# Linear attention on one core: GpSimd's two helper operations tied to VectorE's reciprocal and product of three heads back, with new instruction orders

## The chip, the cores and the metric

The kernel runs on one core of one Trainium2 chip. The metric is the device time of one execution in microseconds. The core has five engines with queues of their own: TensorE (PE, with its weight loads as PEld), VectorE (DVE), ScalarE (ACT), GpSimd (POOL) and SyncE (SP), which here only issues transfers. The profile reports a span from the first to the last instruction, which is not the time.

## The reference, cut to what matters

Inputs q, k, v are bf16 of shape 1 x 32 x 2048 x 128: 32 heads, 2048 rows, 128 columns.

```python
phi_q = where(q > 0, q + 1, exp(q)) + 1e-6
phi_k = where(k > 0, k + 1, exp(k)) + 1e-6
kv  = einsum("bhsd,bhse->bhde", phi_k, v)
z   = einsum("bhsd->bhd", phi_k)
num = einsum("bhqd,bhde->bhqe", phi_q, kv)
den = einsum("bhqd,bhd->bhq", phi_q, z)[..., None] + 1e-6
out = num / den
```

The kernel uses phi(x) = relu(x) + (min(exp(x), 1) + 1e-6) and feeds the two terms to TensorE as two accumulated products.

## The kernel before

A head is 16 tiles of 128 rows. Each engine executes a fixed list of named operations, and a semaphore wait is put before an operation for each dependency in another list. The names, with head `h` (and part) as a suffix:

- ScalarE: `ek` exp(k), `eq` exp(q), `rqa` relu of 8 q tiles, `kvs` copies the kv sums out of PSUM.
- VectorE: `em` and `emq` are min(., 1) + 1e-6 on exp(k) and exp(q); `rkd` is relu of 8 k tiles. All three read and write SBUF. `rqb` is relu of 8 q tiles, `r` the reciprocal of the denominators, `f` the product numerator times reciprocal; these three read PSUM. `r{h}.0` and `f{h}.0` cover 12 tiles, `r{h}.1` and `f{h}.1` four.
- GpSimd: `rkp` is relu of the other 8 k tiles, `v1` copies v beside a column of ones.
- TensorE: `T` transposes q, `kv` is the product of phi(k) and v (below: the v-product), `n` the product of phi(q) and kv.
- SyncE: `ldq`, `ldk`, `ldv` load, `st` stores.

```python
def gate(name, h):          # extra dependencies of v1 and rkp
    return []

ORDER = {
    "DVE": """
        # ... cut ...
        emq8.0 f7.0 rkd10.0 em10.0 r7.1 rqb9 f7.1 r8.0 emq9.0 f8.0 rkd11.0 em11.0 r8.1 rqb10 f8.1 r9.0 rkd12.0 f9.0
        emq10.0 em12.0 r9.1 rqb11 f9.1 r10.0 f10.0 emq11.0 em13.0 rkd13.0 r10.1 rqb12 f10.1 rkd14.0 r11.0 emq12.0
        # ... cut ...
    """,
    "POOL": """
        ident0 ident rkp0.0 rkp1.0 v10.1 v10.0 v11.0 v12.0 rkp2.0 rkp3.0 v13.0 v14.0 rkp5.0 rkp4.0 v15.0 rkp6.0
        # ... cut ...
    """,   # "PE", "ACT" and "SP" likewise
}
# ... cut: inside head(h) ...
add("DVE", f"em{h}.{i}", lambda e, a=a, b=b: e.tensor_scalar(
    em_sb[:, h % NE, a:b], em_sb[:, h % NE, a:b], 1.0, EPS, op0=ALU.min, op1=ALU.add), [f"ek{h}.{i}"])
add("POOL", f"rkp{h}.{i}", lambda e, a=a, b=b: e.tensor_scalar(
    rk_sb[:, h % NR, a:b], k_sb[:, h % NI, a:b], BIG, 0.0, op0=ALU.min, op1=ALU.max),
    over("ldk", h, k_parts, a, b) + freed(NR, h, ("kv", kv_parts)) + gate("rkp", h))
add("POOL", f"v1{h}.{i}", lambda e, a=a, b=b: e.tensor_copy(
    v1_sb[:, h % NV, a:b, 0:D].bitcast(i32), v_sb[:, h % NI, a:b].bitcast(i32)),
    [f"ldv{h}.{i}"] + freed(NV, h, ("kv", kv_parts)) + gate("v1", h))
# ... cut ...
```

Without a gate, `v1` and `rkp` of head h can start when their loads have landed and the v-product of head h - 2 has freed their buffers.

Of the kernel before, what the change touches and what calls it, by code (L numbers as in the profile page):

```python
# [12 lines left out]
HALVES = ((0, 8), (8, 16))  # L13
WHOLE = ((0, 16),)
# [7 lines left out]


def kv_parts(h):
    return WHOLE


RKP = (8, 8, 8, 8, 8, 8, 8, 8, 8, 8, 8, 8, 8, 8, 8, 8, 8, 8, 8, 8, 8, 8, 8, 8, 8, 8, 8, 8, 8, 8, 8, 8)
# [23 lines left out]


def gate(name, h):
    return []


ORDER = {
    "PE": """
        T0.0 T0.1 w1 w0 T1.0 kv0.0 kv1.0 n0.0 n0.1 T2.0 kv2.0 n1.0 T3.0 n1.1 kv3.0 n2.0 T4.0 n2.1 kv4.0 n3.0 T5.0  # L60
        n3.1 kv5.0 n4.0 T6.0 n4.1 kv6.0 n5.0 n5.1 T7.0 kv7.0 n6.0 T8.0 n6.1 kv8.0 n7.0 T9.0 n7.1 kv9.0 n8.0 T10.0
        n8.1 kv10.0 n9.0 T11.0 n9.1 kv11.0 n10.0 T12.0 n10.1 kv12.0 n11.0 T13.0 n11.1 kv13.0 n12.0 T14.0 n12.1
        kv14.0 n13.0 T15.0 n13.1 kv15.0 n14.0 T16.0 n14.1 kv16.0 n15.0 T17.0 n15.1 kv17.0 n16.0 n16.1 T18.0 kv18.0
        n17.0 T19.0 n17.1 kv19.0 n18.0 T20.0 n18.1 kv20.0 n19.0 T21.0 n19.1 kv21.0 n20.0 T22.0 n20.1 kv22.0 n21.0
        T23.0 n21.1 kv23.0 n22.0 T24.0 n22.1 kv24.0 n23.0 n23.1 T25.0 kv25.0 n24.0 T26.0 n24.1 kv26.0 n25.0 T27.0
        n25.1 kv27.0 n26.0 T28.0 n26.1 kv28.0 n27.0 T29.0 n27.1 kv29.0 n28.0 T30.0 n28.1 kv30.0 n29.0 T31.0 n29.1
        kv31.0 n30.0 n30.1 n31.1 n31.0 n31.2
    """,
    "DVE": """
        v1ones0 rkd0.0 em0.1 rkd1.0 rqb0 em0.0 eps0 em1.0 emq0.1 emq0.0 rqb1 v1ones1 eps1 rkd2.0 eps2 ones emq1.0  # L70
        rkd3.0 em2.0 r0.0 f0.0 em3.0 rqb2 r0.1 rkd4.0 f0.1 r1.0 emq2.0 f1.0 em4.0 rkd5.0 r1.1 rqb3 f1.1 r2.0 f2.0
        emq3.0 em5.0 rkd6.0 rqb4 r2.1 f2.1 r3.0 emq4.0 f3.0 em6.0 r3.1 rqb5 rkd7.0 f3.1 r4.0 emq5.0 f4.0 em7.0 r4.1
        f4.1 rqb6 r5.0 f5.0 emq6.0 rkd8.0 em8.0 r5.1 rqb7 f5.1 r6.0 emq7.0 f6.0 rkd9.0 em9.0 r6.1 rqb8 f6.1 r7.0
        emq8.0 f7.0 rkd10.0 em10.0 r7.1 rqb9 f7.1 r8.0 emq9.0 f8.0 rkd11.0 em11.0 r8.1 rqb10 f8.1 r9.0 rkd12.0 f9.0
        emq10.0 em12.0 r9.1 rqb11 f9.1 r10.0 f10.0 emq11.0 em13.0 rkd13.0 r10.1 rqb12 f10.1 rkd14.0 r11.0 emq12.0
# [137 lines left out]
def bass_standalone__linear_attn_elu__prompt_kernel(nc: bass.Bass, q: bass.AP, k: bass.AP, v: bass.AP, out: bass.AP):  # L213
# [11 lines left out]
    with ExitStack() as es:  # L225
# [73 lines left out]
        def head(h):  # L299
# [21 lines left out]
            for i, (a, b) in enumerate(v_parts(h)):  # L321
# [131 lines left out]
```

## Time and profile before

| | before |
|---|---|
| time, runs known at the prediction | 176.82 us median (176.76 to 179.11) |
| the profiled run | 179.61 us, span 177.8, granted clock 0.989 |
| first steady v-product (head 2) to the last (head 31) | 20.99 to 163.97 us, 29 periods |
| steady period where nothing is late | 4.73 us |

"Steady" below means from 21 us on.

The page of the kernel before: busy time of each engine with its share of the span and number of instructions, the rate of the transfers in 40 equal slices, and the chain of work that ended last.

```profile
span 177.8 us, 6416 instructions
...
PE 161.9 (91%) x2842; PEld 158.1 (89%) x2842; DVE 158.4 (89%) x266; ACT 154.4 (87%) x131; POOL 71.5 (40%) x71
...
GB/s 171 323 407 416 411 404 406 412 404 410 408 406 409 406 417 411 407 411 417 412 417 414 420 414 416 416 414 417 412 405 418 414 196 183 285 417 412 418 313 120
...
PE 43%; DVE 20%; DMA 18%; issue 5%; SPq 4%; ACT 4%; POOL 3%; DVEq 0%; POOLq 0%
```

Three engines are within a few per cent of each other, and the chain runs through TensorE more than through any other (43%). The rate falls to 196, 183 and 285 GB/s in three slices near 142 to 156 us. The next view is busy time in one stretch, 130 us of the steady part (columns: stretch, length, then busy us of each engine with its count of instructions, the granted TensorE clock, the share of the transfer engines, GB/s).

```profile
core 0: us, PE busy (x) PEld busy (x) DVE busy (x) ACT busy (x) POOL busy (x), PEclk, DMA share, GB/s
21.00:151.00 130.00, 126.36 (x2272) 124.51 (x2273) 127.74 (x210) 125.56 (x105) 58.45 (x53) 1.00 0.99 397
```

VectorE is the busiest, although it does no more work than 4.6 us per head (its eight operations from start to start). The reason shows in the timeline of the kernel before (start, duration, engine, line, operation, operands; in brackets the idle time before and what ended it). In this kernel L311 is `em`, L314 `rkd`, L318 `rkp`, L352 `rqb`.

```profile
140.29 0.68 DVE L311 TENSOR_SCALAR la<-la 128x2048 bf16<-128x2048 bf16 x1
140.58 1.29 POOL L318 TENSOR_SCALAR la<-la 128x1024 bf16<-128x1024 bf16 x1 [2.42 <-PE la L329]
140.89 1.25 DVE L314 TENSOR_SCALAR la<-la 128x1024 bf16<-128x1024 bf16 x1
...
142.16 0.65 DVE L352 TENSOR_SCALAR la<-la 128x1024 bf16<-128x1024 bf16 x1
```

GpSimd's relu was ready in the middle of `em`. It waited for the rest of it (its record is 1.29 us instead of 1.04), and the following `rkd` took 1.25 us instead of its usual 0.42. `rqb` at 142.16 overlaps the next GpSimd copy and keeps its usual 0.65. Counting every `em`, `emq` and `rkd` that is more than 0.15 us above its usual duration (0.68, 0.68, 0.42), the steady part has 8 of them, together 5.0 us. These are called stretched operations below.

### The profile page before, as it was taken

How to read it: one execution, taken by the hardware profiler on the slowest of the kernel's cores; microseconds unless marked ns; L12 is line 12 of the kernel's file. 1: busy time of each engine (PE TensorE's matmuls, PEld its weight loads, DVE VectorE, ACT ScalarE, POOL GpSimd, SP SyncE). 2: the span in 40 equal slices, each digit the busy share in tenths (PEclk: the TensorE clock that was granted, in tenths of full speed). 3: DMA queues.
4: the chain of work that ended last, by engine and by line, in shares of the span. 5: the costliest groups of instructions: out<-in, count | busy, mean ns of one | idle time of the engine just before them, and what ended most of it. 6: DMA issues, size and time to landing. Idle time of an engine off the chain costs nothing.

```text
span 177.8 us, 6416 instructions
## 1 busy us (share of the span) xinstructions
PE 161.9 (91%) x2842; PEld 158.1 (89%) x2842; DVE 158.4 (89%) x266; ACT 154.4 (87%) x131; POOL 71.5 (40%) x71
## 2 busy tenths in 40 slices
PE   2986999999999999999889999988999989999870
PEld 1976999999999999999789999978999889989770
DVE  0156899999999999998999999999999999989973
ACT  2599799999999999999898999978999979994600
POOL 1253818417454246262723626264256424360000
PEclk9999999999999999999999999999999999999968
DMA  5999999999999999999999999999999945999973
GB/s 171 323 407 416 411 404 406 412 404 410 408 406 409 406 417 411 407 411 417 412 417 414 420 414 416 416 414 417 412 405 418 414 196 183 285 417 412 418 313 120
DMA packets 19179, 67.52 MB, mean 380 GB/s; under 512 B 2128, under 2 KB 2512, under 8 KB 19152
## 3 DMA queue, kind: packets, MB, share of 16 engines
q1 hardware_dynamic: 19152, 67.12, 95.1%
q8 instruction: 22, 0.36, 0.8%
q14 instruction: 5, 0.04, 0.1%
HBM read 50.33 MB, written 16.78 MB: 377 GB/s over the span
## 4 chain that ended last, share of the span: by engine, by line
PE 43%; DVE 20%; DMA 18%; issue 5%; SPq 4%; ACT 4%; POOL 3%; DVEq 0%; POOLq 0%
PE la L329 17%; DMA la<-in_k_dram 11%; PE la L364 9%; PE la L366 8%; PE la L340 8%; DVE la L380 8%; DMA out_dram<-la 7%; SPq L296 4%; DVE la L314 4%; DVE la L311 3%; DVE la L352 2%; ACT la L343 2%; DVE la L345 2%; POOL la L318 2%; POOL la L322 2%
## 5 line engine op out<-in xcount | busy, mean ns | idle before, releaser
L380 DVE TENSOR_TENSOR la<-la 128x1536 bf16<-128x1536 f32 (+2 forms) x65 | 77.7, 1199 | 2.0 <-DMA out_dram<-la 1.4
L366 PE MATMUL la<-la 128*128 128x129 bf16 x512 | 69.2, 222 | 0.0
L364 PE MATMUL la<-la 128*128 128x129 bf16 x512 | 69.1, 221 | 0.0
L329 PE MATMUL la<-la 128*128 128x129 bf16 x1024 | 64.0, 219 | 2.0 <-ACT la L349 1.4
L343 ACT ACTIVATE la<-la 128x2048 bf16<-128x2048 bf16 (+1 forms) x33 | 60.1, 1825 | 6.5 <-PE la L366 6.0
L308 ACT ACTIVATE la<-la 128x2048 bf16<-128x2048 bf16 (+1 forms) x33 | 61.3, 1860 | 2.1 <-DMA la<-in_k_dram 1.9
L329 PEld LDWEIGHTS la<-la 128*128 128x128 bf16 x1024 | 59.9, 97 | 2.7 <-DVE la L278 1.5
L318 POOL TENSOR_SCALAR la<-la 128x1024 bf16<-128x1024 bf16 x32 | 36.1, 1137 | 44.1 <-PE la L329 33.5
L322 POOL COPY la<-la 128x1024 int32<-128x1024 int32 (+1 forms) x33 | 35.3, 1076 | 44.0 <-PE la L329 22.4
L366 PEld LDWEIGHTS la<-la 128*128 128x128 bf16 x512 | 50.0, 98 | 0.0
L364 PEld LDWEIGHTS la<-la 128*128 128x128 bf16 x512 | 47.8, 98 | 0.0
L340 PE MATMUL la<-la 128*128 128x128 bf16 x512 | 34.8, 222 | 7.0 <-DMA la<-in_q_dram 3.6
L340 PEld LDWEIGHTS la<-la 128*128 128x128 bf16 x512 | 29.6, 99 | 9.0 <-issue 4.0
L359 PE MATMUL la<-la 128*128 128x3 bf16 (+1 forms) x192 | 32.6, 170 | 2.5 <-DVE la L380 2.5
L349 ACT ACTIVATE la<-la 128x1024 bf16<-128x1024 bf16 x32 | 32.6, 1019 | 2.5 <-PE la L340 2.5
L311 DVE TENSOR_SCALAR la<-la 128x2048 bf16<-128x2048 bf16 (+1 forms) x33 | 23.3, 706 | 3.1 <-ACT la L308 3.1
L314 DVE TENSOR_SCALAR la<-la 128x1024 bf16<-128x1024 bf16 x32 | 18.0, 566 | 7.4 <-DMA la<-in_k_dram 7.3
L345 DVE TENSOR_SCALAR la<-la 128x2048 bf16<-128x2048 bf16 (+1 forms) x33 | 22.3, 677 | 0.4 <-ACT la L343 0.4
L359 PEld LDWEIGHTS la<-la 128*128 128x128 bf16 x192 | 18.9, 99 | 3.5 <-DVE la L380 3.1
L352 DVE TENSOR_SCALAR la<-la 128x1024 bf16<-128x1024 bf16 x32 | 21.3, 667 | 0.7 <-ACT la L343 0.7
L373 DVE RECIPROCAL la<-la 128x12 f32<-128x12 f32 (+2 forms) x65 | 12.8, 198 | 2.2 <-PE la L366 1.4
L334 ACT ACTIVATE la<-la 128x129 bf16<-128x129 f32 x32 | 9.0, 281 | 1.0 <-PE la L329 1.0
(14 smaller groups left out, 13.5 us busy)
## 6 DMA issues: line engine op xcount, KB each, us to landing
la<-in_k_dram SPq DMA_DIRECT2D x31, 512.0 KB, 13.9
la<-in_q_dram SPq DMA_DIRECT2D x31, 512.0 KB, 13.9
la<-in_v_dram SPq DMA_DIRECT2D x31, 512.0 KB, 13.3
out_dram<-la SPq DMA_DIRECT2D x31, 512.0 KB, 13.2
la<-in_q_dram SPq DMA_DIRECT2D x2, 256.0 KB, 3.0
la<-in_k_dram SPq DMA_DIRECT2D x2, 256.0 KB, 5.2
la<-in_v_dram SPq DMA_DIRECT2D x2, 256.0 KB, 7.6
out_dram<-la SPq DMA_DIRECT2D x2, 192.0 KB, 2.1
```

The lines of the kernel that those rows point to most:

```text
L308: add("ACT", f"ek{h}.{i}", lambda e, a=a, b=b: e.activation(em_sb[:, h % NE, a:b], k_sb[:, h % NI, a:b], ACT.Exp), [f"ldk{h}.{i}"] + freed ...
L311: add("DVE", f"em{h}.{i}", lambda e, a=a, b=b: e.tensor_scalar(em_sb[:, h % NE, a:b], em_sb[:, h % NE, a:b], 1.0, EPS, op0=ALU.min, op1=AL ...
L318: add("POOL", f"rkp{h}.{i}", lambda e, a=a, b=b: e.tensor_scalar(rk_sb[:, h % NR, a:b], k_sb[:, h % NI, a:b], BIG, 0.0, op0=ALU.min, op1=A ...
L322: add("POOL", f"v1{h}.{i}", lambda e, a=a, b=b: e.tensor_copy(v1_sb[:, h % NV, a:b, 0:D].bitcast(i32), v_sb[:, h % NI, a:b].bitcast(i32)), ...
L329: ins = e.matmul(kv_ps, lhsT=src[:, j], rhs=v1_sb[:, h % NV, j, 0:NC], start=(j + part == 0), stop=(j == NT - 1 and part == 1))
L340: ins = e.transpose(xT[:, j], q_sb[:, h % NI, j], ident[:])
L343: add("ACT", f"eq{h}.{i}", lambda e, a=a, b=b: e.activation(emq_sb[:, h % NQ, a:b], xT[:, a:b], ACT.Exp), [f"T{h}.{i}"] + freed(NQ, h, ("n ...
L349: add("ACT", f"rqa{h}", lambda e: e.activation(rq_sb[:, h % NQ, 0:n], xT[:, 0:n], ACT.Relu), over("T", h, q_parts, 0, n) + freed(NQ, h, (" ...
L359: e.matmul(_ap(o_ps[:, :], o + D, [[NC, m]]), lhsT=ones[:], rhs=epsr[:, 0:m], start=True, stop=False, skip_group_check=True)
L364: e.matmul(to, lhsT=emq_sb[:, h % NQ, t], rhs=kvs_sb[:, h % NK], start=False, stop=False, skip_group_check=True)
L366: ins = e.matmul(to, lhsT=rq_sb[:, h % NQ, t], rhs=kvs_sb[:, h % NK], start=False, stop=True, skip_group_check=True)
L380: return e.tensor_tensor(out=_ap(o_sb[:, :, :, :], first(o_sb[:, h % NO, t0, 0:1]) - first(o_sb[:, :, :, :]), [[m * D, nb], [D, m], [1, D] ...
```

## The change

Its apparent intent (the kernel's text does not say): let GpSimd start at a moment when VectorE reads from PSUM, so that the two do not meet. It makes four changes: the gates; the v-product in two halves; GpSimd and the stores in head order; and new orders for all engines.

```diff
 def kv_parts(h):
-    return WHOLE
+    return HALVES
...
 def gate(name, h):
-    return []
+    if h < 3:
+        return []
+    return [f"r{h - 3}.0"] if name == "v1" else [f"f{h - 3}.0"]
...
     "DVE": """
...
-        emq8.0 f7.0 rkd10.0 em10.0 r7.1 rqb9 f7.1 r8.0 emq9.0 f8.0 rkd11.0 em11.0 r8.1 rqb10 f8.1 r9.0 rkd12.0 f9.0
-        emq10.0 em12.0 r9.1 rqb11 f9.1 r10.0 f10.0 emq11.0 em13.0 rkd13.0 r10.1 rqb12 f10.1 rkd14.0 r11.0 emq12.0
+        rkd10.0 emq8.0 f7.0 em10.0 r7.1 rqb9 f7.1 emq9.0 r8.0 rkd11.0 f8.0 em11.0 r8.1 rqb10 f8.1 emq10.0 r9.0
+        rkd12.0 f9.0 em12.0 r9.1 rqb11 f9.1 r10.0 rkd13.0 f10.0 emq11.0 em13.0 r10.1 rqb12 f10.1 r11.0 emq12.0 f11.0
...
     "POOL": """
-        ident0 ident rkp0.0 rkp1.0 v10.1 v10.0 v11.0 v12.0 rkp2.0 rkp3.0 v13.0 v14.0 rkp5.0 rkp4.0 v15.0 rkp6.0
+        ident0 ident v10.0 rkp0.0 v10.1 rkp1.0 v11.0 v12.0 rkp2.0 v13.0 rkp3.0 v14.0 rkp4.0 v15.0 rkp5.0 v16.0
...
     (PE, ACT and SP reordered as well)
```

More of the change, by code (lines that the diff above doesn't have):

```diff
@@ L54, in gate @@
 def gate(name, h):
-    return []
+    if h < 3:
+        return []
+    return [f"r{h - 3}.0"] if name == "v1" else [f"f{h - 3}.0"]
 ORDER = {
     "PE": """
-        T0.0 T0.1 w1 w0 T1.0 kv0.0 kv1.0 n0.0 n0.1 T2.0 kv2.0 n1.0 T3.0 n1.1 kv3.0 n2.0 T4.0 n2.1 kv4.0 n3.0 T5.0
-        n3.1 kv5.0 n4.0 T6.0 n4.1 kv6.0 n5.0 n5.1 T7.0 kv7.0 n6.0 T8.0 n6.1 kv8.0 n7.0 T9.0 n7.1 kv9.0 n8.0 T10.0
-        n8.1 kv10.0 n9.0 T11.0 n9.1 kv11.0 n10.0 T12.0 n10.1 kv12.0 n11.0 T13.0 n11.1 kv13.0 n12.0 T14.0 n12.1
-        kv14.0 n13.0 T15.0 n13.1 kv15.0 n14.0 T16.0 n14.1 kv16.0 n15.0 T17.0 n15.1 kv17.0 n16.0 n16.1 T18.0 kv18.0
-        n17.0 T19.0 n17.1 kv19.0 n18.0 T20.0 n18.1 kv20.0 n19.0 T21.0 n19.1 kv21.0 n20.0 T22.0 n20.1 kv22.0 n21.0
-        T23.0 n21.1 kv23.0 n22.0 T24.0 n22.1 kv24.0 n23.0 n23.1 T25.0 kv25.0 n24.0 T26.0 n24.1 kv26.0 n25.0 T27.0
-        n25.1 kv27.0 n26.0 T28.0 n26.1 kv28.0 n27.0 T29.0 n27.1 kv29.0 n28.0 T30.0 n28.1 kv30.0 n29.0 T31.0 n29.1
-        kv31.0 n30.0 n30.1 n31.1 n31.0 n31.2
+        w1 T0.0 T0.1 w0 kv0.0 T1.0 kv0.1 kv1.0 kv1.1 n0.0 n0.1 T2.0 kv2.0 kv2.1 n1.0 T3.0 n1.1 kv3.0 kv3.1 n2.0 T4.0
+        n2.1 kv4.0 kv4.1 n3.0 T5.0 n3.1 kv5.0 kv5.1 n4.0 T6.0 n4.1 kv6.0 kv6.1 n5.0 n5.1 T7.0 kv7.0 kv7.1 n6.0 T8.0
+        n6.1 kv8.0 kv8.1 n7.0 T9.0 n7.1 kv9.0 kv9.1 n8.0 T10.0 n8.1 kv10.0 kv10.1 n9.0 T11.0 n9.1 kv11.0 kv11.1
+        n10.0 T12.0 n10.1 kv12.0 kv12.1 n11.0 T13.0 n11.1 kv13.0 kv13.1 n12.0 T14.0 n12.1 kv14.0 kv14.1 n13.0 T15.0
+        n13.1 kv15.0 kv15.1 n14.0 T16.0 n14.1 kv16.0 kv16.1 n15.0 T17.0 n15.1 kv17.0 kv17.1 n16.0 T18.0 n16.1 kv18.0
+        kv18.1 n17.0 T19.0 n17.1 kv19.0 kv19.1 n18.0 T20.0 n18.1 kv20.0 kv20.1 n19.0 T21.0 n19.1 kv21.0 kv21.1 n20.0
+        T22.0 n20.1 kv22.0 kv22.1 n21.0 T23.0 n21.1 kv23.0 kv23.1 n22.0 T24.0 n22.1 kv24.0 kv24.1 n23.0 T25.0 n23.1
+        kv25.0 kv25.1 n24.0 T26.0 n24.1 kv26.0 kv26.1 n25.0 n25.1 T27.0 kv27.0 kv27.1 n26.0 T28.0 n26.1 kv28.0
+        kv28.1 n27.0 T29.0 n27.1 kv29.0 kv29.1 n28.0 T30.0 n28.1 kv30.0 kv30.1 n29.0 T31.0 n29.1 kv31.0 kv31.1 n30.0
+        n30.1 n31.0 n31.1 n31.2
@@ L68 @@
     """,
     "DVE": """
-        v1ones0 rkd0.0 em0.1 rkd1.0 rqb0 em0.0 eps0 em1.0 emq0.1 emq0.0 rqb1 v1ones1 eps1 rkd2.0 eps2 ones emq1.0
-        rkd3.0 em2.0 r0.0 f0.0 em3.0 rqb2 r0.1 rkd4.0 f0.1 r1.0 emq2.0 f1.0 em4.0 rkd5.0 r1.1 rqb3 f1.1 r2.0 f2.0
-        emq3.0 em5.0 rkd6.0 rqb4 r2.1 f2.1 r3.0 emq4.0 f3.0 em6.0 r3.1 rqb5 rkd7.0 f3.1 r4.0 emq5.0 f4.0 em7.0 r4.1
-        f4.1 rqb6 r5.0 f5.0 emq6.0 rkd8.0 em8.0 r5.1 rqb7 f5.1 r6.0 emq7.0 f6.0 rkd9.0 em9.0 r6.1 rqb8 f6.1 r7.0
-        emq8.0 f7.0 rkd10.0 em10.0 r7.1 rqb9 f7.1 r8.0 emq9.0 f8.0 rkd11.0 em11.0 r8.1 rqb10 f8.1 r9.0 rkd12.0 f9.0
@@ L75 @@
-        emq10.0 em12.0 r9.1 rqb11 f9.1 r10.0 f10.0 emq11.0 em13.0 rkd13.0 r10.1 rqb12 f10.1 rkd14.0 r11.0 emq12.0
-        f11.0 em14.0 r11.1 rqb13 f11.1 r12.0 f12.0 emq13.0 rkd15.0 em15.0 r12.1 rqb14 f12.1 rkd16.0 r13.0 emq14.0
-        f13.0 em16.0 r13.1 rqb15 f13.1 r14.0 f14.0 emq15.0 em17.0 rkd17.0 r14.1 rqb16 f14.1 r15.0 rkd18.0 f15.0
-        emq16.0 em18.0 r15.1 f15.1 rqb17 r16.0 f16.0 emq17.0 em19.0 rkd19.0 r16.1 rqb18 f16.1 r17.0 emq18.0 f17.0
-        rkd20.0 em20.0 r17.1 rqb19 f17.1 r18.0 f18.0 emq19.0 rkd21.0 em21.0 r18.1 rqb20 f18.1 r19.0 emq20.0 f19.0
@@ L80 @@
-        em22.0 rkd23.0 rkd22.0 rqb21 r19.1 r20.0 f19.1 f20.0 emq21.0 em23.0 rkd24.0 rqb22 r20.1 f20.1 r21.0 emq22.0
-        f21.0 em24.0 rqb23 r21.1 f21.1 r22.0 emq23.0 rkd25.0 f22.0 em25.0 r22.1 f22.1 rqb24 r23.0 f23.0 emq24.0
-        rkd26.0 em26.0 r23.1 rqb25 f23.1 r24.0 emq25.0 f24.0 em27.0 rkd27.0 r24.1 rqb26 f24.1 r25.0 emq26.0 f25.0
-        rkd28.0 em28.0 r25.1 rqb27 f25.1 r26.0 emq27.0 f26.0 rkd29.0 em29.0 r26.1 rqb28 f26.1 r27.0 emq28.0 f27.0
-        rkd30.0 em30.0 r27.1 rqb29 f27.1 r28.0 f28.0 emq29.0 rkd31.0 em31.0 rqb30 r28.1 f28.1 r29.0 emq30.0 f29.0
@@ L85 @@
-        emq31.0 r29.1 rqb31 r30.0 f29.1 f30.0 r30.1 f30.1 r31.1 f31.1 r31.0 r31.2 f31.0 f31.2
+        eps0 ones rkd0.0 v1ones1 v1ones0 rkd1.0 em0.0 emq0.0 eps2 rqb0 eps1 em0.1 em1.0 rqb1 emq0.1 emq1.0 rkd2.0
+        em2.0 rkd3.0 r0.0 f0.0 em3.0 rkd4.0 r0.1 rqb2 f0.1 r1.0 f1.0 emq2.0 em4.0 r1.1 rqb3 f1.1 emq3.0 r2.0 rkd5.0
+        f2.0 em5.0 r2.1 rqb4 f2.1 r3.0 rkd6.0 emq4.0 f3.0 em6.0 r3.1 rqb5 f3.1 r4.0 rkd7.0 f4.0 emq5.0 em7.0 r4.1
+        f4.1 rqb6 emq6.0 r5.0 rkd8.0 f5.0 em8.0 rqb7 r5.1 f5.1 r6.0 emq7.0 rkd9.0 f6.0 em9.0 r6.1 rqb8 f6.1 r7.0
@@ new lines @@
+        rkd10.0 emq8.0 f7.0 em10.0 r7.1 rqb9 f7.1 emq9.0 r8.0 rkd11.0 f8.0 em11.0 r8.1 rqb10 f8.1 emq10.0 r9.0
+        rkd12.0 f9.0 em12.0 r9.1 rqb11 f9.1 r10.0 rkd13.0 f10.0 emq11.0 em13.0 r10.1 rqb12 f10.1 r11.0 emq12.0 f11.0
+        rkd14.0 em14.0 r11.1 rqb13 f11.1 rkd15.0 r12.0 emq13.0 f12.0 em15.0 rqb14 r12.1 f12.1 r13.0 emq14.0 f13.0
+        em16.0 rkd16.0 r13.1 rqb15 f13.1 r14.0 emq15.0 rkd17.0 f14.0 em17.0 r14.1 rqb16 f14.1 r15.0 rkd18.0 emq16.0
+        f15.0 em18.0 r15.1 rqb17 f15.1 r16.0 emq17.0 f16.0 rkd19.0 em19.0 r16.1 rqb18 f16.1 emq18.0 r17.0 rkd20.0
@@ new lines @@
+        f17.0 em20.0 r17.1 rqb19 f17.1 r18.0 rkd21.0 f18.0 emq19.0 em21.0 r18.1 rqb20 f18.1 r19.0 rkd22.0 f19.0
+        emq20.0 em22.0 rqb21 r19.1 f19.1 r20.0 rkd23.0 f20.0 emq21.0 em23.0 rkd24.0 rqb22 r20.1 f20.1 r21.0 f21.0
+        emq22.0 em24.0 r21.1 rqb23 f21.1 r22.0 rkd25.0 f22.0 emq23.0 em25.0 r22.1 rqb24 f22.1 r23.0 emq24.0 f23.0
+        em26.0 rkd26.0 rqb25 r23.1 f23.1 emq25.0 rkd27.0 r24.0 f24.0 em27.0 r24.1 f24.1 rqb26 r25.0 f25.0 emq26.0
+        em28.0 rqb27 r25.1 f25.1 emq27.0 rkd28.0 r26.0 f26.0 em29.0 r26.1 rqb28 f26.1 rkd29.0 r27.0 emq28.0 f27.0
@@ L86 @@
+        em30.0 r27.1 rqb29 f27.1 rkd30.0 r28.0 emq29.0 f28.0 r28.1 rqb30 f28.1 r29.0 emq30.0 em31.0 rkd31.0 f29.0
+        emq31.0 rqb31 r29.1 f29.1 r30.0 f30.0 r30.1 f30.1 r31.0 f31.0 r31.1 f31.1 r31.2 f31.2
     """,
     "ACT": """
-        rqa0 ek0.1 ek0.0 eq0.1 eq0.0 ek1.0 eq1.0 kvs0 rqa1 ek2.0 kvs1 ek3.0 eq2.0 kvs2 rqa2 ek4.0 eq3.0 kvs3 rqa3
+        eq0.0 eq0.1 ek0.0 rqa0 ek1.0 ek0.1 eq1.0 kvs0 ek2.0 kvs1 rqa1 ek3.0 eq2.0 kvs2 rqa2 ek4.0 eq3.0 kvs3 rqa3
         ek5.0 eq4.0 kvs4 rqa4 ek6.0 eq5.0 kvs5 rqa5 ek7.0 eq6.0 kvs6 rqa6 ek8.0 eq7.0 kvs7 rqa7 ek9.0 eq8.0 kvs8
@@ L92 @@
         ek18.0 eq17.0 kvs17 rqa17 ek19.0 eq18.0 kvs18 rqa18 ek20.0 eq19.0 kvs19 rqa19 ek21.0 eq20.0 kvs20 rqa20
-        ek22.0 eq21.0 rqa21 kvs21 ek23.0 eq22.0 kvs22 rqa22 ek24.0 eq23.0 kvs23 rqa23 ek25.0 eq24.0 kvs24 rqa24
+        ek22.0 eq21.0 kvs21 rqa21 ek23.0 eq22.0 rqa22 kvs22 ek24.0 eq23.0 kvs23 rqa23 ek25.0 eq24.0 kvs24 rqa24
         ek26.0 eq25.0 kvs25 rqa25 ek27.0 eq26.0 kvs26 rqa26 ek28.0 eq27.0 kvs27 rqa27 ek29.0 eq28.0 kvs28 rqa28
@@ L97 @@
     "POOL": """
-        ident0 ident rkp0.0 rkp1.0 v10.1 v10.0 v11.0 v12.0 rkp2.0 rkp3.0 v13.0 v14.0 rkp5.0 rkp4.0 v15.0 rkp6.0
-        v16.0 v17.0 v18.0 rkp7.0 rkp8.0 rkp9.0 v19.0 rkp10.0 v110.0 rkp11.0 v111.0 v112.0 rkp13.0 rkp12.0 v113.0
-        v114.0 rkp15.0 rkp14.0 v115.0 rkp16.0 v117.0 v116.0 rkp17.0 rkp18.0 v119.0 v118.0 rkp19.0 rkp20.0 v121.0
-        v120.0 rkp21.0 v122.0 rkp23.0 rkp22.0 v123.0 rkp24.0 v124.0 v125.0 v126.0 rkp25.0 rkp26.0 rkp27.0 v127.0
-        rkp28.0 v128.0 rkp29.0 v129.0 rkp30.0 rkp31.0 v130.0 v131.0
+        ident0 ident v10.0 rkp0.0 v10.1 rkp1.0 v11.0 v12.0 rkp2.0 v13.0 rkp3.0 v14.0 rkp4.0 v15.0 rkp5.0 v16.0
@@ L103 @@
+        rkp6.0 v17.0 rkp7.0 v18.0 rkp8.0 v19.0 rkp9.0 v110.0 rkp10.0 v111.0 rkp11.0 v112.0 rkp12.0 v113.0 rkp13.0
+        v114.0 rkp14.0 v115.0 rkp15.0 v116.0 rkp16.0 v117.0 rkp17.0 v118.0 rkp18.0 v119.0 rkp19.0 v120.0 rkp20.0
+        v121.0 rkp21.0 v122.0 rkp22.0 v123.0 rkp23.0 v124.0 rkp24.0 v125.0 rkp25.0 v126.0 rkp26.0 rkp27.0 v127.0
+        v128.0 rkp28.0 v129.0 rkp29.0 v130.0 rkp30.0 v131.0 rkp31.0
     """,
     "SP": """
-        ldq0.0 ldq0.1 ldk0.0 ldk0.1 ldk1.0 ldq1.0 ldv0.1 ldv0.0 ldv1.0 ldk2.0 ldv2.0 ldk3.0 ldq2.0 ldv3.0 ldq3.0
@@ L106 @@
-        ldk4.0 ldq8.0 ldv4.0 ldk5.0 ldq4.0 ldv5.0 ldk6.0 ldk7.0 ldq5.0 ldv6.0 ldq6.0 ldv8.0 ldk8.0 ldv7.0 ldq7.0
-        ldk9.0 ldq9.0 ldk11.0 ldq12.0 ldq11.0 ldv9.0 ldk10.0 ldq10.0 ldk14.0 ldv10.0 ldq13.0 ldk15.0 ldk12.0 ldv11.0
-        ldk13.0 ldv13.0 ldv12.0 ldv15.0 ldv14.0 st0.0 ldq14.0 ldq17.0 ldq16.0 ldv16.0 ldq15.0 ldq18.0 ldk16.0
-        ldq19.0 ldv20.0 ldv17.0 ldk18.0 st1.0 st2.0 ldk17.0 st4.0 ldk19.0 ldv19.0 ldv18.0 st3.0 ldv21.0 ldv22.0
-        st5.0 st6.0 st10.0 ldk20.0 ldk22.0 ldv23.0 ldq20.0 ldk21.0 ldq21.0 st9.0 ldk23.0 st7.0 ldq22.0 st8.0 ldq23.0
@@ L111 @@
-        ldk24.0 ldv25.0 ldq26.0 ldq27.0 ldk25.0 ldv24.0 ldk26.0 ldq24.0 st11.0 ldk27.0 ldv26.0 ldq28.0 ldq25.0
-        st14.0 ldq30.0 st12.0 ldv27.0 ldk28.0 st13.0 ldk29.0 ldv28.0 st15.0 ldk30.0 st17.0 ldv29.0 ldq29.0 st18.0
-        st25.0 ldv30.0 ldk31.0 st16.0 ldv31.0 st21.0 ldq31.0 st23.0 st20.0 st24.0 st27.0 st26.0 st28.0 st19.0 st22.0
-        st29.0 st30.0 st31.1 st31.0 st31.2
+        ldq0.0 ldq0.1 ldk0.0 ldv0.0 ldk0.1 ldk1.0 ldv0.1 ldq1.0 ldv1.0 ldk2.0 ldv2.0 ldk3.0 ldq2.0 ldk4.0 ldq3.0
@@ new lines @@
+        ldv3.0 ldv4.0 ldk5.0 ldq4.0 ldv5.0 ldk6.0 ldv6.0 ldq5.0 ldk7.0 ldq6.0 ldk8.0 ldv7.0 ldq7.0 ldq8.0 ldk9.0
+        ldv8.0 ldv9.0 ldk10.0 ldq9.0 ldv10.0 ldq10.0 ldk11.0 ldk12.0 ldv11.0 ldv12.0 ldq11.0 ldv13.0 ldq12.0 st0.0
+        ldv14.0 ldq13.0 ldk13.0 st1.0 ldv15.0 ldk14.0 ldk15.0 ldk16.0 ldq14.0 ldv16.0 ldv17.0 ldk17.0 ldq15.0
+        ldv18.0 st2.0 ldk18.0 ldq16.0 ldq17.0 ldq18.0 st3.0 ldq19.0 st4.0 st5.0 st6.0 ldv19.0 ldq20.0 ldk19.0
+        ldk20.0 ldv20.0 ldk21.0 ldv21.0 ldq21.0 ldv22.0 ldk22.0 st7.0 ldv23.0 ldk23.0 ldq22.0 ldv24.0 ldk24.0 st8.0
@@ L115 @@
+        ldv25.0 st9.0 ldk25.0 ldq23.0 ldq24.0 st10.0 ldk26.0 ldq25.0 st11.0 ldk27.0 ldv26.0 ldq26.0 ldv27.0 st12.0
+        ldk28.0 st13.0 st14.0 ldq27.0 ldv28.0 ldk29.0 st15.0 ldk30.0 ldq28.0 ldv29.0 st16.0 ldq29.0 ldv30.0 ldq30.0
+        st17.0 ldk31.0 ldv31.0 ldq31.0 st18.0 st19.0 st20.0 st21.0 st22.0 st23.0 st24.0 st25.0 st26.0 st27.0 st28.0
+        st29.0 st30.0 st31.0 st31.1 st31.2
     """,
```

## The prediction

> **What bounds the kernel now.** In the steady state a head takes 4.73 us (timeline). TensorE and ScalarE are both 10.0 of 10 us busy between 50 and 80 us (busy time by stretch), so both set this period. VectorE is hardly looser: its eight operations, start to start, add to about 4.6 us. The first steady v-product starts at 20.99 us, after q of head 2 has landed (about 19.8); the last, of head 31, at 164.13. Twenty-nine periods of 4.725 are 137.0, measured 143.1: 6.1 us are lost. The tail from there is 13.7. Where the 6.1 went: VectorE blocked by GpSimd, seen as relu(k) of 1.26 us instead of 0.42 (90.66, 120.88, 140.89) and em or emq of 1.1 instead of 0.68 (85.24, 137.60, 148.04, 159.91), eight in all, about 5 us; products waiting for an output store, 0.86 and 0.53; and the transfer queue, which stood 15.7 us on stores issued too early (the slices at 142 to 156 us move 196, 183 and 285 GB/s instead of 410), so that k of head 31 lands at 156.9 and TensorE and ScalarE lose about 2.
>
> The Trainium skill, "SBUF — State Buffer", section "Who interferes with whom": VectorE and GpSimd share a port pair; who issues first holds it for the whole instruction. The trace agrees: 0.83 us lost per relu(k) against a GpSimd operation of 1.04. It also shows who wins: where GpSimd arrives in the middle of one such VectorE operation and another follows directly (8.75, 115.14, 140.58), GpSimd goes next and the second is blocked.
>
> **What the change does.** No arithmetic is added; kv comes in halves. Stores are issued in head order, after their data are ready: the transfer hole (about 2.4 us) and the store waits (1.4) should go. The start is bound by the same tenth transfer (q of head 2), so it gains little. The gates start the v copy at the end of a 12-tile reciprocal and relu(k) at the end of the 12-tile product. Where one SBUF-to-SBUF operation stands there, followed by work from PSUM, the copy (1.04) hides under the product (1.67) and relu(k) under reciprocal, relu(q), 4-tile product (1.27). But in the new order two such operations stand in a row in 17 places from head 3 on (after r3, r6, r7, r14, r15; after f4, f10, f11, f13, f16, f18 to f23, f25): there the gate puts GpSimd exactly between them, an estimated 0.84 us each, up to 14 us, against VectorE's slack of about 0.13 per head. With none of these collisions the sum is 21 + 137 + 13.7 = 171.7 profiled (170.7 timed); with all of them about 183. A searched order would hardly keep 17 at full price, so I stand between.
>
> **Predicted: 175.5 us, range 170 to 182. Chances: faster by over 2% 0.36, within 2% 0.42, slower by over 2% 0.22.**
>
> **What would show it.** Right: no transfer slice under 390 GB/s between 10 and 150 us; no product waiting for a store; GpSimd waiting for VectorE, not TensorE; the v copies inside the 12-tile products; em, emq or relu(k) stretched by about 0.84 at the 17 places, more VectorE busy time than 158.4. Wrong: VectorE's em, emq, relu(k) all at 0.68, 0.69, 0.42, so GpSimd yields; then the time is near 171.
>
> **What would make it wrong.** GpSimd waking later or yielding (faster); TensorE waiting for a late v1 or relu(k) half (slower); late v loads in the first ten heads.

## The result, and the profile after

The changed kernel takes 184.61 us median (184.51 to 184.76, 4 runs) against 177.13 for the kernel before in the same rounds: a ratio of 1.0399, 95% interval 1.032 to 1.0478, slower. A ratio here is the mean time of one kernel's fast runs over that of the other's fast runs of the same rounds, so it is not quite the ratio of the medians. All runs of the changed kernel were at a granted clock of 0.997 or more.

The page of the changed kernel, the same parts as before:

```profile
span 182.8 us, 6466 instructions
...
PE 163.9 (90%) x2842; PEld 158.3 (87%) x2842; DVE 166.8 (91%) x266; ACT 155.2 (85%) x131; POOL 81.7 (45%) x71
...
GB/s 160 293 414 413 406 408 410 411 405 406 410 405 419 412 411 412 414 410 417 416 415 406 420 412 420 409 417 418 414 419 415 415 420 414 353 177 118 118 185 161
...
DVE 68%; ACT 10%; issue 9%; PE 6%; DMA 4%; SPq 1%; DVEq 0%
DVE la L384 30%; DVE la L349 10%; DVE la L315 9%; DVE la L356 8%; ACT la L347 6%; DVE la L318 6%; DVE la L377 4%; DMA la<-in_k_dram 4%; PE la L344 2%; ACT la L312 2%; ACT la L353 2%; SPq L300 1%; PE la L333 1%; PE la L368 1%; PE la L370 1%
```

The hole in the transfers is gone, and after the first two the slices stay above 400 GB/s until the last load has landed at 152.2 us. But VectorE has 8.4 us more busy time with the same 266 instructions, and the chain of work now runs through VectorE for 68% of the span (20% before). Busy time in the same stretch of 130 us:

```profile
core 0: us, PE busy (x) PEld busy (x) DVE busy (x) ACT busy (x) POOL busy (x), PEclk, DMA share, GB/s
21.00:151.00 130.00, 121.29 (x2150) 117.47 (x2148) 129.32 (x200) 119.86 (x101) 64.67 (x52) 1.00 1.03 413
```

VectorE is busy for 129.3 of 130 us and finishes 200 instructions where it finished 210 before; TensorE has fallen from 126.4 to 121.3 us. The waits of GpSimd in the changed kernel (us in total, times, longest) show that the gates are what it now waits for; L326 is `v1`, L322 `rkp`, L377 the reciprocal, L384 the product:

```profile
POOL la L326 <- DVE la L377: 38.5, 25, 3.1
POOL la L322 <- DVE la L384: 33.1, 27, 4.6
POOL la L326 <- DMA la<-in_v_dram: 12.0, 4, 6.3
POOL la L326 <- PE la L333: 1.6, 1, 1.6
```

The timeline of the changed kernel at `f10.0 emq11.0 em13.0`; L349 is `emq`, L315 `em`, L356 `rqb`:

```profile
69.69 1.74 DVE L384 TENSOR_TENSOR la<-la 128x1536 bf16<-128x1536 f32 x1
71.35 0.68 DVE L349 TENSOR_SCALAR la<-la 128x2048 bf16<-128x2048 bf16 x1
71.52 1.41 POOL L322 TENSOR_SCALAR la<-la 128x1024 bf16<-128x1024 bf16 x1 [0.85 <-DVE la L384]
71.95 1.53 DVE L315 TENSOR_SCALAR la<-la 128x2048 bf16<-128x2048 bf16 x1
73.40 0.17 DVE L377 RECIPROCAL la<-la 128x4 f32<-128x4 f32 x1
73.49 0.65 DVE L356 TENSOR_SCALAR la<-la 128x1024 bf16<-128x1024 bf16 x1
```

The product ends at 71.43 and opens the gate. By then `emq` has started (71.35), so GpSimd waits. When `emq` is done, GpSimd goes next and `em`, the second operation in the row, takes 1.53 us instead of 0.68. Such stretched operations number 18 in the steady part, together 15.1 us; 17 of them stand exactly at the 17 places the prediction lists, at 0.83 to 0.85 us each, and the eighteenth (at 25.97 us) is behind f1.

Put together, the 182.8 us are 19.6 to the v-product of head 2, 150.6 from there to that of head 31 (170.21), and 12.6 after it. Before, the same three were 21.0, 143.0 and 13.8. TensorE's v-product never waits for GpSimd in the changed kernel's list of waits, so the gates do not cost by making TensorE's inputs late.

### The profile page after: what moved, and what is told of

It reads as the page before. It is cut to its first block, busy times and chain, and to the rows that moved or that the text cites. A ratio compares the mean times of both kernels' runs of the same rounds, so it can differ in the third digit from the quotient of the medians.

```text
span 182.8 us, 6466 instructions
## 1 busy us (share of the span) xinstructions
PE 163.9 (90%) x2842; PEld 158.3 (87%) x2842; DVE 166.8 (91%) x266; ACT 155.2 (85%) x131; POOL 81.7 (45%) x71
## 4 chain that ended last, share of the span: by engine, by line
DVE 68%; ACT 10%; issue 9%; PE 6%; DMA 4%; SPq 1%; DVEq 0%
DVE la L384 30%; DVE la L349 10%; DVE la L315 9%; DVE la L356 8%; ACT la L347 6%; DVE la L318 6%; DVE la L377 4%; DMA la<-in_k_dram 4%; PE la L344 2%; ACT la L312 2%; ACT la L353 2%; SPq L300 1%; PE la L333 1%; PE la L368 1%; PE la L370 1%
## 5 line engine op out<-in xcount | busy, mean ns | idle before, releaser
L384 DVE TENSOR_TENSOR la<-la 128x1536 bf16<-128x1536 f32 (+2 forms) x65 | 77.8, 1197 | 0.7
L347 ACT ACTIVATE la<-la 128x2048 bf16<-128x2048 bf16 (+1 forms) x33 | 60.1, 1825 | 16.0 <-PE la L370 11.1
L370 PE MATMUL la<-la 128*128 128x129 bf16 x512 | 68.0, 220 | 0.0
L368 PE MATMUL la<-la 128*128 128x129 bf16 x512 | 67.9, 219 | 0.0
L333 PE MATMUL la<-la 128*128 128x129 bf16 x1024 | 64.2, 219 | 2.1 <-ACT la L338 0.8
L326 POOL COPY la<-la 128x1024 int32<-128x1024 int32 (+1 forms) x33 | 38.2, 1160 | 52.0 <-DVE la L377 38.5
L322 POOL TENSOR_SCALAR la<-la 128x1024 bf16<-128x1024 bf16 x32 | 43.0, 1345 | 33.1 <-DVE la L384 33.1
L315 DVE TENSOR_SCALAR la<-la 128x2048 bf16<-128x2048 bf16 (+1 forms) x33 | 31.9, 970 | 1.0 <-ACT la L312 1.0
L353 ACT ACTIVATE la<-la 128x1024 bf16<-128x1024 bf16 x32 | 32.6, 1018 | 0.0
L318 DVE TENSOR_SCALAR la<-la 128x1024 bf16<-128x1024 bf16 x32 | 16.7, 522 | 8.1 <-DMA la<-in_k_dram 8.1
L349 DVE TENSOR_SCALAR la<-la 128x2048 bf16<-128x2048 bf16 (+1 forms) x33 | 23.9, 727 | 0.0
L356 DVE TENSOR_SCALAR la<-la 128x1024 bf16<-128x1024 bf16 x32 | 21.2, 664 | 1.1 <-ACT la L347 1.1
L377 DVE RECIPROCAL la<-la 128x12 f32<-128x12 f32 (+2 forms) x65 | 12.7, 195 | 1.3 <-ACT la L338 1.0
```

The lines of the kernel that those rows point to most:

```text
L333: ins = e.matmul(kv_ps, lhsT=src[:, j], rhs=v1_sb[:, h % NV, j, 0:NC], start=(j + part == 0), stop=(j == NT - 1 and part == 1))
L347: add("ACT", f"eq{h}.{i}", lambda e, a=a, b=b: e.activation(emq_sb[:, h % NQ, a:b], xT[:, a:b], ACT.Exp), [f"T{h}.{i}"] + freed(NQ, h, ("n ...
L349: add("DVE", f"emq{h}.{i}", lambda e, a=a, b=b: e.tensor_scalar(emq_sb[:, h % NQ, a:b], emq_sb[:, h % NQ, a:b], 1.0, EPS, op0=ALU.min, op1 ...
L368: e.matmul(to, lhsT=emq_sb[:, h % NQ, t], rhs=kvs_sb[:, h % NK], start=False, stop=False, skip_group_check=True)
L370: ins = e.matmul(to, lhsT=rq_sb[:, h % NQ, t], rhs=kvs_sb[:, h % NK], start=False, stop=True, skip_group_check=True)
L384: return e.tensor_tensor(out=_ap(o_sb[:, :, :, :], first(o_sb[:, h % NO, t0, 0:1]) - first(o_sb[:, :, :, :]), [[m * D, nb], [D, m], [1, D] ...
```

## The experiments

"Gates at the start" means the change's gates. All runs that could be built gave correct results. Times are medians, each with its four runs unless stated; the kernel before, run beside them on the same chip, had medians of 178.13, 176.81, 177.73 and 177.17 in the four sets. The medians are over all runs, the ratios over fast runs alone: e3, e8 and e12 had one slow run each, and the medians of their fast runs are 214.38, 180.51 and 188.39. The mean granted clock of the fast runs was 0.97 or more, except in e3 (0.943 to 0.955). Collisions are counted in one profile of each.

| run | time us | ratio to before (95%) | stretched operations, their sum us |
|---|---|---|---|
| before | 177.13 | 1 | 8, 5.0 |
| after | 184.61 | 1.040 (1.032 to 1.048) | 18, 15.1 |
| e1_no_gates | 185.36 | 1.045 (1.037 to 1.052) | 29, 15.8 |
| e2_gate_at_run_end | 173.35 | 0.977 (0.970 to 0.984) | 0 |
| e6_one_in_row | 174.57 | 0.983 (0.976 to 0.990) | 2, 1.2 |
| e7_half_repaired | 179.58 | 1.012 (1.005 to 1.018) | 11, 8.8 |
| e9_order_and_end | 174.03 | 0.978 (0.973 to 0.983) | 1, 0.6 |
| e3_before_gated | 214.56 | 1.206 (1.195 to 1.216) | 30, 21.5 |
| e12_pool_sorted | 188.45 | 1.053 (1.040 to 1.066) | 25, 15.1 |
| e3b_gated_pool_sorted | 190.59 | 1.070 (1.063 to 1.077) | 23, 19.1 |
| e10b_end_pool_sorted | 175.06 | 0.986 (0.979 to 0.993) | 2, 1.0 |
| e4_before_sp | 178.76 | 1.008 (1.001 to 1.015) | 11, 6.3 |
| e5_kv_whole | 190.04 | 1.069 (1.063 to 1.075) | 18, 15.1 |
| e8_relu_in_two | 181.42 | 1.020 (1.011 to 1.030) | 19, 10.5 |

**The theory.** VectorE's `em`, `emq`, `rkd` and any GpSimd operation exclude each other, and where GpSimd is waiting when one of them ends, GpSimd goes before the next one. The gates of the change open at the head of a row of such operations, so the first runs and the second is blocked for about one GpSimd operation. **The rivals.** The new orders or the halved v-product are slow by themselves; or any gate costs, because it delays GpSimd and so TensorE.

### Take the gates away: e1_no_gates

```diff
 def gate(name, h):
-    if h < 3:
-        return []
-    return [f"r{h - 3}.0"] if name == "v1" else [f"f{h - 3}.0"]
+    return []
```

> The changed kernel with both gates taken away and every order kept. Lock theory (the gates put GpSimd between two neighbouring VectorE operations at 17 places): those 17 are no longer forced, some collisions come by chance, as in the kernel before; 174 to 181 us, VectorE busy time below 164 us, and GpSimd waits for TensorE and transfers again. Rival (the new orders or the halved v-product are slow by themselves, the gates are harmless): 183 to 186 us.

Measured 185.36 us. **A miss.** Of the operations stretched at the 17 places two still are (`rkd16` and `rkd26`), the other 15 are not, but other collisions have come for them. The timeline of this run (L324 is `v1`, L320 `rkp`, L347 `emq`, L313 `em`):

```profile
72.60 0.68 DVE L313 TENSOR_SCALAR la<-la 128x2048 bf16<-128x2048 bf16 x1
72.63 1.55 POOL L324 COPY la<-la 128x1024 int32<-128x1024 int32 x1 [2.49 <-PE la L331]
...
74.15 1.04 POOL L320 TENSOR_SCALAR la<-la 128x1024 bf16<-128x1024 bf16 x1
...
74.61 1.12 DVE L347 TENSOR_SCALAR la<-la 128x2048 bf16<-128x2048 bf16 x1
```

With GpSimd's list sorted by head and no gate, copy and relu start back to back when a v-product ends, and these two microseconds meet VectorE about once per head: 29 stretched operations of 0.18 to 0.87 us, in sum 15.8, as much as the gates cost. So by the time alone the run looks like the first rival, and only the durations show that the cause is the same lock. The sentence "the gates made it slow" is therefore not right; the gates moved the collisions, without lowering their sum. That these collisions, and not the orders as such, make this run slow is shown by the next run, which keeps the orders.

### Move the gates to the end of the row: e2_gate_at_run_end

The orders of all engines stay as the change has them.

```diff
+    dve = ORDER["DVE"].split()
+    i = dve.index(f"r{h - 3}.0" if name == "v1" else f"f{h - 3}.0")
+    while dve[i + 1].startswith(("em", "rkd")):
+        i += 1
+    return [dve[i]]
-    return [f"r{h - 3}.0"] if name == "v1" else [f"f{h - 3}.0"]
```

> The changed kernel with every order kept; each gate is moved from the reciprocal or product to the last SBUF-to-SBUF operation of the row that follows it, so that GpSimd starts beside work that reads PSUM. Lock theory: no em, emq or relu(k) from head 3 on is stretched, VectorE busy about 152 to 154 us, span about 170 to 172 us, timed 172 to 174. Rival (any gate costs, for it delays GpSimd and so TensorE): 182 to 187, since GpSimd is now started even later.

Measured 173.35 us, span 171.8, VectorE 153.0 us busy, no stretched operation. The same place in the timeline of this run (L353 `emq`, L319 `em`, L326 `rkp`, L360 `rqb`, L388 the products):

```profile
69.40 0.68 DVE L353 TENSOR_SCALAR la<-la 128x2048 bf16<-128x2048 bf16 x1
70.00 0.68 DVE L319 TENSOR_SCALAR la<-la 128x2048 bf16<-128x2048 bf16 x1
70.77 1.04 POOL L326 TENSOR_SCALAR la<-la 128x1024 bf16<-128x1024 bf16 x1 [1.84 <-DVE la L319]
...
70.88 0.66 DVE L360 TENSOR_SCALAR la<-la 128x1024 bf16<-128x1024 bf16 x1
71.45 0.68 DVE L388 TENSOR_TENSOR la<-la 128x512 bf16<-128x512 f32 x1
```

`rkp` now starts after both SBUF operations and runs beside `rqb` and the 4-tile product, and neither side waits. Busy time in the stretch of 130 us, this run:

```profile
21.00:151.00 130.00, 129.88 (x2354) 128.85 (x2352) 127.41 (x217) 129.63 (x109) 57.10 (x55) 1.00 1.03 413
```

TensorE and ScalarE are full again (129.9 and 129.6 of 130), and all engines have finished more instructions. Only the moment at which GpSimd is released differs from the changed kernel, and it is worth 11.3 us (the two were timed in different sets; against the kernel before, 0.977 and 1.040). Rival two (a gate costs because it is late) fails: this gate is later. Rival one (the new orders or the halves are slow by themselves) fails as well: both are in this run.

This run also gives the cost of the collisions without the start and the end. Its three parts are 20.6, 138.6 and 12.6 us; in the changed kernel the middle one is 150.6, so the collisions cost 12.0 us there, of the 15.1 us by which operations are stretched.

### Mend VectorE's order, keep the gates: e6_one_in_row and e7_half_repaired

```diff
-    r10.0 rkd13.0 f10.0 emq11.0 em13.0 r10.1 rqb12 f10.1 r11.0 emq12.0 f11.0 rkd14.0 em14.0 r11.1 ...
+    r10.0 rkd13.0 f10.0 em13.0 r10.1 rqb12 f10.1 emq12.0 r11.0 rkd14.0 f11.0 em14.0 r11.1 rqb13 f11.1 emq13.0 ...
```

e6 does this for heads 2 to 29, e7 from head 16 on.

> The changed kernel with its gates kept and only VectorE's order mended: from head 2 to 29 every row is reciprocal, relu(k), 12-tile product, em, reciprocal, relu(q), 4-tile product, emq, so one SBUF-to-SBUF operation stands where a gate opens. Lock theory: none of the 17 stretched operations is left, VectorE busy 152 to 154 us, timed 172 to 174 us. Rival (gates cost): 182 to 186.

> As the run with one operation in a row, but mended only from head 16 on: 9 of the 17 places stay. Lock theory, 0.84 us each less VectorE's slack of about 0.13 per free head: nine stretched operations and about 176 to 179 us, between the other two. Rival: no change from 184.6, or all of the gain.

e6: 174.57 us, VectorE 153.4 us busy; of the 17 none is left (the two stretched operations stand at 26.8 and 139.9 us). e7: 179.58 us with 11 stretched operations, of which nine are the predicted places that stay. Both are 0.6 us above the expected range, and they order as the number of stretched operations does: 2, 11, 18 give 174.6, 179.6, 184.6. From 2 to 18 that is 10.0 us for 16 operations, 0.63 us each, less than the 0.84 by which each is stretched. The prediction's argument is that VectorE's slack against the period of 4.73 us, 0.13 us per head, takes up the rest. Over 29 heads that is 3.8 us, against the 3.1 us (15.1 less 12.0) found with e2; that it is this slack which takes them up is argued, not shown.

### Both repairs: e9_order_and_end

e6's order with e2's gate.

> Both repairs in the changed kernel: one SBUF-to-SBUF operation in a row in VectorE's order, and the gates on that operation. Each repair alone gave 173.4 and 174.6 us. Lock theory: nothing left to gain on collisions (none against 0 and 2), so 172.5 to 174.5 us, the period of TensorE and ScalarE is the bound. Rival: the two gains add, below 170.

Measured 174.03 us in six runs (173.64 to 174.16). The gains do not add, as expected: once nothing is stretched, the period of TensorE and ScalarE is the bound (in the stretch of 130 us they are busy 129.9 and 129.6 us in e2, 128.3 and 128.1 in e9). e2 and e9 both beat both kernels, the one before by 2.2 to 2.3% (95%: 1.6 to 3.0% and 1.7 to 2.7%).

### The same with the orders of the kernel before: e3, e12, e3b, e10b

These ask whether the cure and the disease depend on the change's orders. e3 adds only the gates to the kernel before:

```diff
 def gate(name, h):
-    return []
+    if h < 3:
+        return []
+    return [f"r{h - 3}.0"] if name == "v1" else [f"f{h - 3}.0"]
```

> The kernel before, all its orders kept, with the change's two gates added. Its VectorE order has 23 places where two or three SBUF-to-SBUF operations follow a gate directly (after f1, f2, f5 to f10, f12, f14 to f20, f23 to f28 and r22). Lock theory, 0.84 us each: about 20 stretched operations in place of 8, VectorE busy 168 to 171 us, timed 184 to 190 us. Rival (gates do neither good nor harm): 177 to 178.

Measured 214.56 us, far above the range: a miss by size. The number of stretched operations is larger than expected too (30), but there is a second cost, seen in the waits of this run (L331 is the v-product, L320 and L324 GpSimd's two):

```profile
PE la L331 <- POOL la L320: 17.4, 6, 3.9
...
PE la L331 <- POOL la L324: 7.1, 4, 3.6
```

The old GpSimd list is not in head order (`rkp5.0 rkp4.0`), so an operation held back by a later gate holds up the one behind it, which TensorE needs. The profile of this run fell in the slow state, so these waits and its 30 collisions are quoted for their kind, not their size. What share of the 214.56 us comes from the late GpSimd operations, from the collisions and from the lower clock (0.943 to 0.955 in the fast runs) is not separated. So GpSimd's list was sorted, as the change has it, with all other lists left:

```diff
     "POOL": """
-        ident0 ident rkp0.0 rkp1.0 v10.1 v10.0 v11.0 v12.0 rkp2.0 rkp3.0 v13.0 v14.0 rkp5.0 rkp4.0 v15.0 rkp6.0
+        ident0 ident v10.0 rkp0.0 v10.1 rkp1.0 v11.0 v12.0 rkp2.0 v13.0 rkp3.0 v14.0 rkp4.0 v15.0 rkp5.0 v16.0
...
```

and run without gates (e12), with gates at the start of the row (e3b), and with gates at its end (e10b). A first try of gates at the end without the sorting, e10_before_end_gate, was refused at the build: its waits formed a deadlock (`rkp5` waits for an operation that needs `rkp4`, which stands behind it). Its expectation was

> The kernel before, all its orders kept, with each gate put on the last SBUF-to-SBUF operation of the row after the reciprocal or product. Lock theory: no stretched operation in the steady heads, VectorE busy about 152 to 154 us; the transfer hole at 142 to 156 us stays, so 173 to 176 us. Rival: 177 to 178, or slower because GpSimd's own order is shuffled here and a late gate delays its next operation.

The three that ran:

> The kernel before with GpSimd's order sorted by head and no gates: the control for the two gated runs of this order (190.6 us with gates at the row's start, 175.1 at its end). If the gates at the row's end made the gain, this run must not have it: v copy and relu(k) then start back to back when the v-product two heads back ends, as in the changed kernel without gates (185.4), about one stretched operation per head, 178 to 186 us. Rival (the sorting made the gain): 173 to 176 us with few stretched operations.

> The kernel before with the change's two gates and with GpSimd's order alone sorted by head, as the changed kernel has it; the first try without the sorting gave 214.6 us because late gates held up the operations behind them on GpSimd. Lock theory: about 21 stretched operations of 0.84 us, VectorE busy 168 to 171, 185 to 192 us. Rival: the 214.6 was a matter of GpSimd's order alone, and now it is 176 to 179.

> As the run before it in this list (kernel before, GpSimd sorted by head), with each gate on the last SBUF-to-SBUF operation of the row. Lock theory: no or few stretched operations, VectorE busy 152 to 155, 173 to 176 us with the old order of TensorE, VectorE, ScalarE and transfers. Rival: as slow as its partner, since both have the same number of gates.

| gates | orders of the change | orders of before, GpSimd sorted |
|---|---|---|
| none | 185.36 | 188.45 |
| at the start of the row | 184.61 | 190.59 |
| at its end | 173.35 | 175.06 |

In both columns, no gate and a gate at the start of the row are alike, and the gate at its end takes 11 to 16 us off. e3b has 23 stretched operations where about 21 were expected, and VectorE is busy 172.2 us (168 to 171 expected). e12 lies 2.5 us above its range. The sorting alone does not help, it costs 5%. e10b lies in its range. The kernel before, unsorted and ungated, had only 8 collisions; no run separates how its GpSimd list avoided the others.

### The transfers: e4_before_sp

The kernel before with the changed kernel's SP list and nothing else.

```diff
     "SP": """
-        ldq0.0 ldq0.1 ldk0.0 ldk0.1 ldk1.0 ldq1.0 ldv0.1 ldv0.0 ldv1.0 ldk2.0 ldv2.0 ldk3.0 ldq2.0 ldv3.0 ldq3.0
+        ldq0.0 ldq0.1 ldk0.0 ldv0.0 ldk0.1 ldk1.0 ldv0.1 ldq1.0 ldv1.0 ldk2.0 ldv2.0 ldk3.0 ldq2.0 ldk4.0 ldq3.0
...
```

> The kernel before with the changed kernel's order of transfers and nothing else. The prediction's terms: the hole in the transfers at 142 to 156 us goes (2.4 us) and the products wait for no store (1.4 us), so 173 to 175 us; the eight collisions stay near eight. Rival: without the hole nothing moves (177 to 178), because VectorE bounds the kernel before.

Measured 178.76 us, ratio 1.008: **a miss**, and the rival is right. The rate of the transfers in this run:

```profile
GB/s 152 276 418 410 413 406 408 408 406 408 407 411 411 413 416 406 413 413 413 417 413 411 415 413 416 417 408 422 415 416 416 413 421 416 411 411 277 156 199 156
```

The hole is gone and no product waits for a store, yet the time did not fall. The stretched operations rose from 8 (5.0 us) to 11 (6.3), presumably since earlier or later loads also move the starts of GpSimd. The difference of 1.3 us does not account for all of the expected 3.8; that the old hole lay behind VectorE's delays rather than before them is argued, not shown. Two traces support it. e10b keeps the old order of transfers: its queue still stands 12.6 us on stores, its slices still dip to 320 and 293 GB/s and a product still waits 1.1 us for a store, yet head 2 to head 31 takes 139.1 us against 138.6 in e2. And the 4.4 us by which the kernel before is longer there (143.0) are no more than its 5.0 us of stretched operations.

### The halves of the v-product: e5_kv_whole

```diff
 def kv_parts(h):
-    return HALVES
+    return WHOLE
     (and kv{h}.1 taken out of TensorE's list)
```

> The changed kernel with the v-product of a head in one part again, gates and orders kept. Both the lock theory and the prediction: VectorE bounds it, the halves cost nothing and save nothing, 184 to 186 us with the same 18 stretched operations. Rival (the halves cost TensorE a step per head): under 183.

Measured 190.04 us: **a miss**. The same 18 stretched operations of 15.1 us are there, and head 2 to head 31 takes 150.3 us as in the changed kernel (150.6), but the v-product of head 2 starts at 25.51 instead of 19.62. The wait is in ScalarE's timeline of this run, where L345 is `eq1` and L342 the transposes `T1`:

```profile
17.15 1.88 ACT L345 ACTIVATE la<-la 128x2048 bf16<-128x2048 bf16 x1 [4.78 <-PE la L342]
```

With a whole first v-product, the transposes of head 1 stand behind it, and it cannot begin before both halves of k are through. In the changed kernel `eq1` starts at 12.78. So the halves are worth some 5 us, all of it in the first 26 us, given these orders. (The kernel before has no halves and starts at 20.99, with another order on TensorE.) They are no cause of the slowdown.

### Halve what GpSimd holds: e8_relu_in_two

```diff
 def rkp_parts(h):
-    return ((16 - RKP[h], 16),) if RKP[h] else ()
+    return ((8, 12), (12, 16))
     (rkp{h}.1 put right behind rkp{h}.0 in GpSimd's list)
```

> The changed kernel, gates and orders kept, with GpSimd's relu(k) cut into two operations of four tiles each. Lock theory (held for one whole instruction, then the waiting side goes): at the 12 places after a product the blocked operation waits for a piece of about 0.6 us instead of 1.04, so it is stretched by about 0.4 instead of 0.84; 179 to 181 us, and the five places after a reciprocal stay at 0.84. Rival (GpSimd's total work sets the price): unchanged or slower than 184.6.

The fast runs took 179.91, 180.51 and 182.34 us (a fourth, of 231.42, was slow at a clock of 0.662). The only profile fell in that slow run, so it is read for VectorE's and GpSimd's durations alone, which agree with the fast profiles. The same place as above (L351 `emq`, L324 `rkp`, L317 `em`):

```profile
89.40 0.68 DVE L351 TENSOR_SCALAR la<-la 128x2048 bf16<-128x2048 bf16 x1
89.57 2.00 POOL L324 TENSOR_SCALAR la<-la 128x512 bf16<-128x512 bf16 x2 [0.86 <-DVE la L386]
90.00 1.10 DVE L317 TENSOR_SCALAR la<-la 128x2048 bf16<-128x2048 bf16 x1
```

`em` now takes 1.10 us, stretched by 0.42 instead of 0.84. That is the case at every one of the 12 places behind a product, while the five behind a reciprocal stay at 0.83 to 0.84. GpSimd's records add up to more (91.9 us busy in that run, waiting included, against 81.7), and by its fast runs the kernel is faster than the changed one (1.020 against 1.040 to before). So the price is set by the length of the one operation that is let through.

## Why the prediction was right or wrong

- **Right: what would be lost, and where.** Seventeen places of about 0.84 us were listed; all 17 were found, at 0.83 to 0.85. VectorE's busy time rose above 158.4, GpSimd waits for VectorE, and no product waits for a store, as listed. "With all of them about 183" does not say whether it is a span or a time; the span is 182.8, the time 184.61.
- **Wrong, the step that failed:** "A searched order would hardly keep 17 at full price, so I stand between." The predicted 175.5 lies 4.8 us above the time without collisions (170.7). The runs showed the full price at every place: the collisions cost 12.0 us (head 2 to head 31 takes 150.6 us, and 138.6 in e2, where the same orders run with nothing stretched). So this term was 7.2 us too small. The argument from the trace was set aside for a guess about the order. There was no evidence in the profile for a reduction, and the place lists, gates and lock together left none.
- **Wrong, a term mis-sized:** the step from span to time. The prediction took 1.0 us off ("171.7 profiled (170.7 timed)"), apparently because it compared one run's span (177.8) with the median of other runs (176.82). The profiled run was itself 179.61 us, and the time is 1.8 us more than the span in every run. This term was 2.8 us too small.
- **The sum without collisions was met, in part by luck:** 171.7 was predicted as a span and e2 has 171.8. But its parts were off in opposite directions: 137 for the heads, measured 138.6, and 34.7 for start and tail, measured 33.2.
- **Not borne out: the gain from the transfers.** "The transfer hole (about 2.4 us) and the store waits (1.4) should go" is true of the profile, but e4 shows no gain in time from it (ratio 1.008). Waits of a queue were added to the sum beside VectorE's losses as if both lay on one chain.
- **Right by the number:** "The start is bound by the same tenth transfer (q of head 2), so it gains little": the v-product of head 2 moved from 20.99 to 19.62. This q landed at 19.67 before and at 18.54 after, and its transposes started at 19.77 and 18.73; but TensorE was busy with the products of head 0 until then in both, so the trace does not tell which of the two bound it. The halves of the v-product, given half a line, turned out to carry the start with these orders (e5: q of head 2 had landed at 18.99, yet the v-product started at 25.51).
- **Not foreseen:** that the changed orders without gates lose just as much (e1). The prediction called the gates' place the cost, and had no count for the ungated kernel.
- **On the skill.** "SBUF — State Buffer", section "Who interferes with whom", says "Issue order, not op shape, decides who blocks." The trace agrees: `em` takes 0.68 or 1.53 us with the same operands. That work from PSUM does not meet GpSimd fits "VectorE: DVE Perf Modes", section "Mode 2×_2P — use both read ports for one tensor", by which the mode that uses the second port needs SBUF operands; here `rqb` keeps 0.65 to 0.66 us beside GpSimd.

## What to carry to other kernels

When two engines exclude each other per operation, list what the busier one does directly after the event that releases the other: if two contending operations follow, the waiting engine goes between them and the second pays for one whole operation. Release it at the end of such a row, not at its start; here this one move was worth 11 us and made the same orders 2.3% faster than the kernel before (95%: 1.6 to 3.0%). When a count from the trace gives a number, keep it as the prediction until something measured speaks against it, and convert spans to times with the pair of one and the same run.

## What the Trainium skill lacked or had wrong

- "SBUF — State Buffer", section "Who interferes with whom", says that whoever issues first holds the port pair for the whole instruction, but not who goes next when one engine waits and the other has a further operation ready. The runs show the waiting GpSimd going before VectorE's next operation at all 17 places of the changed kernel, so that the second of two VectorE operations in a row took 1.53 us instead of 0.68 (or 1.26 instead of 0.42).
- The same section gives no price for a VectorE operation behind a blocked GpSimd one. Here it is 0.84 us for a GpSimd operation of 1.04, and 0.42 where GpSimd's operation was cut in two.
- No page names the remedy of releasing GpSimd by a semaphore at the end of VectorE's row of SBUF operations (173.35 against 184.61 us).
